# Two MLP tiles of three chunks first, a reordered opening, and loads in order of need, in a fused attention and MLP kernel

## The chip, the cores and the metric

The kernel runs on one core of a Trainium2 chip. The metric is the device time of one execution in microseconds. Most executions of one kernel agree within a few tenths of a per cent, but some fall into a slower state. The word "span" is the length of one profiled execution, and it is about 2 us shorter than the time.

The five engines have these names in the profile: PE is the matrix engine (TensorE), PEld its weight load, DVE is VectorE, ACT is ScalarE and POOL is GpSimd. SP (SyncE) issues some of the DMAs.

## The reference

Lightning attention with a decay for each head, in blocks of 64 positions, feeds a two-layer MLP with an ELU between its layers.

```python
# q, k, v: [B=4, H=8, S=768, D=64];  w_in: [512, 2048];  w_out: [2048, 512]
for b in range(nb):                                # blocks along S, kv_state carried
    intra = (qb @ kb.T) * Dmask                    # lam ** (i - j) where i >= j, else 0
    intra = intra @ vb
    inter = (qb * lam_pow) @ kv_state
    out[..., block, :] = intra + inter
    kv_state = lam_block * kv_state + (kb * rev_pow).T @ vb
x = out.transpose(0, 2, 1, 3).reshape(3072, 512)
h = x @ w_in
g = where(h > 0, h, exp(min(h, 0)) - 1)
return g @ w_out                                   # [3072, 512], float32
```

## The kernel before

The kernel takes blocks of 128 positions, which gives the same result. A "chunk" is 128 of the 3072 rows of `x`, so there are 24 chunks, 6 for each of the 4 sequences (`NCB = 6`). The MLP works on tiles of 2 to 4 chunks. A tile is 16 "slots", one for each 128 columns of the hidden layer. One slot is: the first matmul `mm1` into PSUM; `exp` and `relu` of it on ScalarE; `g = min(e - 1, r)` on VectorE; and, two slots later (`LAG = 2`), the second matmul `mm2`. The attention of the next tile's chunks is put between these, in given slots.

```python
TILES = [3, 4, 4, 4, 4, 3, 2]          # chunks of each MLP tile
# G1 = 3: chunks of tile 0.  G2 = 7: chunks of tiles 0 and 1.  NB = 8: buffers of q, k, v
...
def att_kd(g, eng):                    # k * decay; on GpSimd from tile 2 on
    ...
    kd = asb.tile([128, H, 64], FP16, tag="kd", name=f"kd{g}", bufs=3)
    ...
        eng.tensor_tensor(out=dst, in0=src, in1=ks[:]..., op=ALU.mult)

def att_q(g):                          # q * decay, in place, on GpSimd
    qt = nats[g][0]
    nc.gpsimd.tensor_tensor(out=qt[:], in0=qt[:], in1=qp[:]..., op=ALU.mult)

def att_T_dma(g):                      # transposes of q and k by DMA, from tile 2 on
    qt = asb.tile([128, NHP, 128], FP16, tag="qT", name=f"qT{g}", bufs=3)
    z = asb.tile([128, NHP, 2, 128], FP16, tag="kz", name=f"kz{g}", bufs=3)
    nc.sync.dma_start_transpose(out=qt[:], in_=nats[g][0][:]...)
    nc.sync.dma_start_transpose(out=z[:]..., in_=kn[g % NB][:]...)
...
def elu(s, e, r):                      # both inputs are in SBUF
    nc.vector.scalar_tensor_tensor(
        out=g[:, :w], in0=e, scalar=-1.0, in1=r, op0=ALU.add, op1=ALU.min)
...
for t in range(2, NMT):                # chunks from tile 2 on
    for c in range(TILES[t]):
        g, f = T0[t] + c, (t - 1) * NFT + off + step * c       # f: slot of its attention
        regular(g, f)
        prep.append((f - 6, lambda g=g: (att_q(g), att_kd(g, nc.gpsimd), att_T_dma(g))))
        prep.append((f - 16, lambda g=g: emit_load(g)))
# the other weight and chunk loads are put in `prep` at slots -3 and -2
...
for i in range(NB):                    # before slot 0
    nc.scalar.memzero(kn[i][:, :, 1:3, :])
```

The tiles `kn[i]` hold k with a zero half beside each head, so that one transpose gives a zero-padded result. Loads write the even parts and the `memzero` writes the rest. All loads that cast to 16 bits are issued by GpSimd. A load into `kn`, `vz` or `qn` has to wait until the chunk that used this buffer eight chunks earlier is done with it.

## Time and profile before

| | before |
|---|---|
| median time | 243.7 us (243.2 to 244.4) |
| span of the profiled execution | 241.3 us |
| PE busy | 212.7 us (88%) |
| first `exp` of slot 16 | 65.5 us |

From the page of before: the first line is the busy time of each engine with its share of the span and its instruction count. Each of the others has 40 equal slices of the span (6.03 us each); a digit is a share in tenths.

```profile
PE 212.7 (88%) x1444; PEld 120.5 (50%) x1444; DVE 164.8 (68%) x381; ACT 147.6 (61%) x335; POOL 121.1 (50%) x146
...
PE   1377799960989999999999999999999999999992
...
PEclk9999999996799999999999999999999999999999
DMA  6999999999999997977999999318830009200302
```

PE is full from the eleventh slice on. Before that it has one hole, in the ninth and tenth slices, and in this hole the granted clock (PEclk) falls.

The table of stretches of before gives each engine's busy time in a stretch of the span. The last three lines are tiles 1 to 3, more or less.

```profile
core 0: us, PE busy (x) PEld busy (x) DVE busy (x) ACT busy (x) POOL busy (x), PEclk, DMA share, GB/s
...
55.00:60.00 5.00, 0.13 (x2) 0.13 (x3) 0.00 (x0) 0.19 (x1) 5.00 (x7) 0.64 1.85 139
...
65.00:99.00 34.00, 32.94 (x224) 17.73 (x223) 27.69 (x62) 20.16 (x38) 29.60 (x33) 1.00 1.62 140
99.00:132.00 33.00, 32.99 (x222) 17.60 (x221) 25.79 (x55) 21.37 (x46) 17.72 (x19) 1.00 1.11 114
132.00:165.00 33.00, 32.77 (x213) 17.12 (x210) 22.42 (x45) 21.73 (x47) 16.16 (x18) 1.00 1.10 115
```

The hole in the opening comes from GpSimd's queue of loads. The timeline of POOL in before has the start, the length, the engine, the line, the operation and, in brackets, the idle time before it and what ended that. GpSimd's multiplies for chunk 7 come behind the last weight load, at 51.4 us:

```profile
50.51 0.88 POOL L108 DMA_DIRECT2D vz_78<-in_v_dram  x1 [0.75 <-DMA wo_7_133<-in_moe_w_out_dram]
51.41 1.06 POOL L233 TENSOR_TENSOR qn_409<-qn_409,qp 128x512 f16<-128x512 f16 x1
52.42 1.04 POOL L225 TENSOR_TENSOR kd_668<-kn_92,ks 128x512 f16<-128x512 f16 x1
```

The DMA transpose of that chunk follows, and PE waits for it, as the timeline of PE in before shows:

```profile
59.87 0.39 PE L333 MATMUL psSU_0_885<-qT_670,kz_671 128*128 128x128 f16 x2 [5.88 <-DMA kz_671<-kn_92]
```

From 82 us on the two multiplies of a chunk do not stand together, though twice `kd` of one chunk and `q` of the next do, as here at 118.05. Timeline of POOL in before, and below it timeline of DVE in before:

```profile
114.16 1.09 POOL L233 TENSOR_TENSOR qn_1471<-qn_1471,qp 128x512 f16<-128x512 f16 x1
118.05 1.04 POOL L225 TENSOR_TENSOR kd_1768<-kn_85,ks 128x512 f16<-128x512 f16 x1 [2.80 <-PE psSU_3_1694 L339]
119.05 1.49 POOL L233 TENSOR_TENSOR qn_1591<-qn_1591,qp 128x512 f16<-128x512 f16 x1
120.49 0.94 POOL L108 DMA_DIRECT2D qn_1885<-in_q_dram  x1
```

### The profile page before, as it was taken

What the parts mean: (1) busy time and instruction counts of PE and PEld (TensorE: products, weight loads), DVE (VectorE), ACT (ScalarE), POOL (GpSimd) and SP (SyncE); (2) the same over time, 40 slices, a digit from 0 to 9 for tenths busy, and PEclk for the clock granted to TensorE, in tenths of its full rate; (3) what the DMA queues carried; (4) which work ended last, traced back from release to release, by engine and by line L of the source; (5) the groups of instructions that cost most, each with busy time, mean ns of one, the idle gap of its engine ahead of it and who ended that gap; (6) DMA issues with size and microseconds to landing.
All of it is one profiled execution on the core that took longest, in us unless ns stands there. A gap on an engine that the chain in (4) does not pass through costs nothing.

```text
span 241.3 us, 4272 instructions
## 1 busy us (share of the span) xinstructions
PE 212.7 (88%) x1444; PEld 120.5 (50%) x1444; DVE 164.8 (68%) x381; ACT 147.6 (61%) x335; POOL 121.1 (50%) x146
## 2 busy tenths in 40 slices
PE   1377799960989999999999999999999999999992
PEld 0266565640545555555555455555455545555660
DVE  7465698770697887667888886548776739654542
ACT  6728666571265665687555656777556575667771
POOL 7987869789999885307578646053400000000000
PEclk9999999996799999999999999999999999999999
DMA  6999999999999997977999999318830009200302
GB/s 44 119 157 175 193 158 199 179 147 131 146 161 208 154 101 74 128 220 101 53 100 105 114 230 149 65 17 56 244 62 4 0 0 216 26 0 3 130 1 87
DMA packets 112373, 26.89 MB, mean 111 GB/s; under 512 B 103136, under 2 KB 109280, under 8 KB 112352
## 3 DMA queue, kind: packets, MB, share of 16 engines
q0 software_dynamic: 81552, 13.64, 79.1%
q1 hardware_dynamic: 30800, 12.99, 27.8%
q8 instruction: 11, 0.18, 0.3%
q14 instruction: 10, 0.08, 0.1%
HBM read 27.27 MB, written 6.29 MB: 139 GB/s over the span
## 4 chain that ended last, share of the span: by engine, by line
PE 67%; DMA 13%; POOL 10%; DVE 5%; issue 3%; ACT 1%; SPq 0%; DVEq 0%; ACTq 0%; POOLq 0%
DMA vz_82<-in_v_dram 4%; DMA wo_7_133<-in_moe_w_out_dram 4%; DMA wo_1_127<-in_moe_w_out_dram 4%; DMA kz_671<-kn_92 2%; PE psM_3_1503 L436 1%; PE psM_1_1026 L436 1%; PE psM_1_2416 L436 1%; PE psM_3_2418 L436 1%; PE psM_1_1501 L436 1%; PE psM_2_1502 L436 1%; PE psM_2_2417 L436 1%; PE psM_2_1027 L436 1%; PE psM_0_1500 L436 1%; PE psM_3_1028 L436 1%; PE psM_0_2415 L436 1%
## 5 line engine op out<-in xcount | busy, mean ns | idle before, releaser
L409 PEld LDWEIGHTS <-wi_7_125 128*128 128x128 f16 x56 | 5.7, 102 | 6.3 <-issue 0.9
L409 PEld LDWEIGHTS <-wi_1_119 128*128 128x128 f16 x56 | 5.3, 97 | 6.7 <-issue 2.1
L409 PEld LDWEIGHTS <-wi_3_121 128*128 128x128 f16 x56 | 5.4, 98 | 5.3
L409 PEld LDWEIGHTS <-wi_5_123 128*128 128x128 f16 x56 | 5.4, 98 | 5.3
L409 PEld LDWEIGHTS <-wi_4_122 128*128 128x128 f16 x56 | 5.4, 98 | 5.0
L409 PEld LDWEIGHTS <-wi_2_120 128*128 128x128 f16 x56 | 5.3, 98 | 4.8
L409 PEld LDWEIGHTS <-wi_6_124 128*128 128x128 f16 x56 | 5.3, 98 | 4.8
L409 PEld LDWEIGHTS <-wi_0_118 128*128 128x128 f16 x56 | 5.3, 98 | 4.7
L225 POOL TENSOR_TENSOR kd_1650<-kn_92,ks 128x512 f16<-128x512 f16 x1 | 1.0, 1042 | 11.0 <-PE psSU_3_1577 L339 11.0
L225 POOL TENSOR_TENSOR kd_2450<-kn_90,ks 128x512 f16<-128x512 f16 x1 | 1.0, 1042 | 10.8 <-issue 10.8
L333 PE MATMUL psSU_0_885<-qT_670,kz_671 128*128 128x128 f16 x2 | 0.4, 300 | 5.9 <-DMA kz_671<-kn_92 5.9
L414 ACT ACTIVATE e_903<-psH_898 128x384 f32<-128x384 f32 x1 | 0.5, 490 | 7.8 <-PE psH_898 L409 7.8
L260 PE MATMUL psT_193<-ident_138,qn_134 128*128 128x128 f16 x4 | 0.6, 308 | 5.1 <-DMA qn_134<-in_q_dram 5.1
L108 POOL DMA_DIRECT2D kn_92<-in_k_dram x6 | 4.5, 764 | 0.8 <-DMA wi_2_120<-in_moe_w_in_dram 0.6
L225 POOL TENSOR_TENSOR kd_2653<-kn_91,ks 128x512 f16<-128x512 f16 x1 | 1.0, 1043 | 6.8 <-issue 6.8
L345 DVE TENSOR_TENSOR pp_0_889<-psSU_0_885,mask 128x256 f16<-128x256 f32 x1 | 0.4, 425 | 5.8 <-PE psSU_0_885 L339 5.8
L374 PEld LDWEIGHTS <-vz_79 128*128 128x128 f16 x24 | 2.6, 112 | 2.8 <-issue 0.9
L333 PEld LDWEIGHTS <-kz_671 128*128 128x128 f16 x8 | 0.7, 114 | 6.1 <-DMA kz_671<-kn_92 6.1
L374 PEld LDWEIGHTS <-vz_84 128*128 128x128 f16 x24 | 2.3, 98 | 2.8 <-DVE xt_583 L395 0.5
L374 PEld LDWEIGHTS <-vz_81 128*128 128x128 f16 x24 | 2.3, 98 | 2.5
L374 PEld LDWEIGHTS <-vz_80 128*128 128x128 f16 x24 | 2.3, 98 | 2.5
L374 PEld LDWEIGHTS <-vz_82 128*128 128x128 f16 x24 | 2.3, 98 | 2.5
(1734 smaller groups left out, 881.8 us busy)
## 6 DMA issues: line engine op xcount, KB each, us to landing
vz_77<-in_v_dram POOLq DMA_DIRECT2D x3, 128.0 KB, 5.5
vz_78<-in_v_dram POOLq DMA_DIRECT2D x3, 128.0 KB, 5.1
vz_79<-in_v_dram POOLq DMA_DIRECT2D x3, 128.0 KB, 4.9
vz_80<-in_v_dram POOLq DMA_DIRECT2D x3, 128.0 KB, 6.2
vz_81<-in_v_dram POOLq DMA_DIRECT2D x3, 128.0 KB, 6.8
vz_82<-in_v_dram POOLq DMA_DIRECT2D x3, 128.0 KB, 8.7
kn_92<-in_k_dram POOLq DMA_DIRECT2D x6, 64.0 KB, 5.6
vz_84<-in_v_dram POOLq DMA_DIRECT2D x3, 128.0 KB, 5.4
```

What stands on the lines that cost most here:

```text
L108: nc.gpsimd.dma_start(out=dst, in_=src[:, rows].rearrange("h p d -> p h d"))
L225: eng.tensor_tensor(out=dst, in0=src, in1=ks[:].rearrange("p (g t) -> p g t", t=2).unsqueeze(3) .broadcast_to([128, NHP, 2, 64]), op=ALU.mult,
L260: nc.tensor.transpose(pt[:, j, hp, :], in_=src[:, 2 * hp : 2 * hp + 2, :], identity=ident16[:])
L333: nc.tensor.matmul(pu[:, hh * 128 : (hh + 1) * 128], lhsT=z[:, hp, hh, :], rhs=qt[:, hp, :], start=True, stop=True,)
L345: nc.vector.tensor_tensor(out=P[:], in0=pu[:, 0:256].rearrange("p (h i) -> p h i", h=2), in1=mask[:, 2 * hp : 2 * hp + 2, :], op=ALU.mult,)
L374: nc.tensor.matmul(po[:, hp, :], lhsT=vt[:, b0 : b0 + 2, :], rhs=P[:, hh, :], start=(hh == 0), stop=(hh == 1 and cb == 0), skip_group_chec ...
L409: nc.tensor.matmul(pH[:, :w], lhsT=wi[:, kk, j * 128 : (j + 1) * 128], rhs=xt[m][:, kk, :w], start=(kk == 0), stop=(kk == NHP - 1),)
L414: nc.scalar.activation(e[:, :w], pH[:, :w], AF.Exp)
L436: nc.tensor.matmul(psM[m][i][:], lhsT=g[:, i * 128 : (i + 1) * 128], rhs=wo16[wof[n][0]][:, wof[n][1], :], start=(n == 0), stop=(n == NFT ...
```

## The change

Its intent: reach the dense part sooner, by loading in the order of need and by sharing the opening's copies between ScalarE and VectorE; then let GpSimd prepare further ahead, with five buffers in place of three. The core of the diff:

```diff
-    TILES = [3, 4, 4, 4, 4, 3, 2]
+    TILES = [3, 3, 4, 4, 4, 4, 2]              # so G2 is 6
...                                             # loads, all at the start of GpSimd's queue:
-    emit_load(1)
-    emit_load(2)
+    emit_load(1, (0, 1)); emit_load(0, (2,)); emit_load(2, (0, 1)) ...
     emit_w_load(0)
     emit_load(3)
+    emit_w_load(1); emit_w_load(2); emit_load(4); emit_w_load(3); emit_w_load(4)
+    emit_load(5)
+    for i in range(5, 8):
+        emit_w_load(i)
+    emit_load(6)
+    emit_load(7)
...                                             # kd, qT (twice), kz:
-            kd = asb.tile([128, H, 64], FP16, tag="kd", name=f"kd{g}", bufs=3)
+            kd = asb.tile([128, H, 64], FP16, tag="kd", name=f"kd{g}", bufs=5)
...                                             # state of a sequence's first chunk:
-                nc.scalar.copy(new[r, r], u)
+                nc.vector.tensor_copy(new[r, r], u)
...                                             # stores, issued LAG + 2 slots later:
-                nc.sync.dma_start(out=out[t0 : t0 + 128, :], in_=o[:])
+                stores.append((s + LAG + 2, out[t0 : t0 + 128, :], o))
...
+    def pool_work(g):
+        if g + 2 < NG:
+            emit_load(g + 2)
+        att_q(g)
+        att_kd(g, nc.gpsimd)
+        att_T_dma(g)
...
-            prep.append((f - 6, lambda g=g: (att_q(g), att_kd(g, nc.gpsimd), att_T_dma(g))))
-            prep.append((f - 16, lambda g=g: emit_load(g)))
+            prep.append((f - 6, lambda g=g: pool_work(g)))
+    for i in range(NB):
+        prep.append((i, lambda i=i: nc.scalar.memzero(kn[i][:, :, 1:3, :])))
...                                             # before slot 0:
-    for i in range(NB):
-        nc.scalar.memzero(kn[i][:, :, 1:3, :])
```

Cut from it: the order of transposes, copies and mask in the opening, the PSUM tags of tile 2's attention, and the slots of each chunk. The zeroing of `kn[i]` now stands in slot `i`, behind the loads of k in the order of the program.

More of the change, by code (lines that the diff above doesn't have):

```diff
@@ L64 @@
     nc.sync.dma_start(out=lam_b[:], in_=lam.unsqueeze(0).broadcast_to([128, H]))
+    ident16 = cpool.tile([128, 128], FP16, name="ident16")
+    nc.vector.memset(ident16[:], 0.0)
+    causT = cpool.tile([128, 128], FP32, name="causT")
+    nc.vector.memset(causT[:], 1.0)
     vz = [cpool.tile([128, 2 * H, 64], FP16, name=f"vz_{i}") for i in range(NB)]
@@ L79 @@
         nc.vector.memset(kz0[i][0:64, :, 1, :], 0.0)
-    for i in range(NB):
+    for i in range(G1):
         nc.vector.memset(vz[i][:, 1::2, :], 0.0)
-    def late_zeros():
-        for i in range(G1):
-            nc.vector.memset(kdz[i][:, :, 1:3, :], 0.0)
-        for hp in range(NHP):
-            for i in range(2):
-                nc.vector.memset(st[hp][i][:], 0.0)
+        nc.vector.memset(kdz[i][:, :, 1:3, :], 0.0)
     nats = {}
@@ L132 @@
     emit_load(0, (0, 1))
-    ident16 = cpool.tile([128, 128], FP16, name="ident16")
-    nc.gpsimd.memset(ident16[:], 0.0)
     nc.gpsimd.affine_select(
@@ L138 @@
     )
-    causT = cpool.tile([128, 128], FP32, name="causT")
-    nc.gpsimd.memset(causT[:], 1.0)
     nc.gpsimd.affine_select(
@@ L148 @@
     nc.gpsimd.iota(iota_r[:], pattern=[[1, 128]], base=0, channel_multiplier=0)
+    emit_load(1, (0, 1))
     emit_load(0, (2,))
-    emit_load(1)
-    emit_load(2)
+    emit_load(2, (0, 1))
+    emit_load(1, (2,))
+    emit_load(2, (2,))
     emit_w_load(0)
     emit_load(3)
+    emit_w_load(1)
+    emit_w_load(2)
+    emit_load(4)
+    emit_w_load(3)
+    emit_w_load(4)
+    emit_load(5)
[3 more added lines that the diff above has]
+    emit_load(7)
     loglam = cpool.tile([128, H], FP32, name="loglam")
@@ L181, with emit_mask @@
     mask = cpool.tile([128, H, 128], FP32, name="mask")
-    nc.vector.tensor_tensor(
-        out=mask[:],
-        in0=causT[:].unsqueeze(1).broadcast_to([128, H, 128]),
-        in1=dn[:].unsqueeze(2).broadcast_to([128, H, 128]),
-        op=ALU.mult,
-    )
+    def emit_mask():
+        nc.vector.tensor_tensor(
+            out=mask[:],
+            in0=causT[:].unsqueeze(1).broadcast_to([128, H, 128]),
+            in1=dn[:].unsqueeze(2).broadcast_to([128, H, 128]),
+            op=ALU.mult,
+        )
     qs = cpool.tile([128, NHP, 128], FP32, name="qs")
@@ L238, in att_T_dma @@
     def att_T_dma(g):
-        qt = asb.tile([128, NHP, 128], FP16, tag="qT", name=f"qT{g}", bufs=3)
-        z = asb.tile([128, NHP, 2, 128], FP16, tag="kz", name=f"kz{g}", bufs=3)
+        qt = asb.tile([128, NHP, 128], FP16, tag="qT", name=f"qT{g}", bufs=5)
+        z = asb.tile([128, NHP, 2, 128], FP16, tag="kz", name=f"kz{g}", bufs=5)
         nc.sync.dma_start_transpose(out=qt[:], in_=nats[g][0][:].rearrange("p h d -> p (h d)"))
@@ L265, in att_ev @@
         pt = psT.pop(g)
-        qt = asb.tile([128, NHP, 128], FP16, tag="qT", name=f"qT{g}", bufs=3)
+        qt = asb.tile([128, NHP, 128], FP16, tag="qT", name=f"qT{g}", bufs=5)
         z = kz0[g % 2]
@@ L271, in att_ev @@
             nc.scalar.copy(out=qt[:], in_=pt[:, 0])
-        for hh in range(2):
-            r = slice(hh * 64, (hh + 1) * 64)
-            nc.scalar.copy(out=z[r, :, hh, :], in_=pt[r, 1])
+        nc.scalar.copy(out=z[0:64, :, 0, :], in_=pt[0:64, 1])
+        if g < G1:
+            nc.vector.tensor_copy(z[64:128, :, 1, :], pt[64:128, 1])
+        else:
+            nc.scalar.copy(out=z[64:128, :, 1, :], in_=pt[64:128, 1])
         qkT[g] = (qt, z)
@@ L401, with emit_stores @@
     psM = {}
+    stores = []
+    def emit_stores(s):
+        while stores and stores[0][0] <= s:
+            _, dst, o = stores.pop(0)
+            nc.sync.dma_start(out=dst, in_=o[:])
     def mm1(s):
@@ L457, in regular @@
     def regular(g, f):
+        tags = ("psSU", "psM3") if T0[2] <= g < T0[3] else ("psSU", "psSU")
         for hp in range(NHP):
-            at(f + hp, lambda hp=hp: att_SU(g, hp))
+            at(f + hp, lambda hp=hp: att_SU(g, hp, tags[hp % 2]))
             at(f + 1 + hp, lambda hp=hp: att_PI(g, hp), late=hp == 0)
@@ L469, in short @@
         at(f + 2, lambda: att_X(g, 2))
-    for g, (ft, f) in zip(range(G1, G2), ((-1, 1), (3, 5), (7, 9))):
+    for g, ft, f in ((3, 0, 2), (4, 5, 7), (5, 10, 12)):
         at(ft, lambda g=g: (att_T_pe(g), att_ev(g)))
-        regular(g, f)
+        (short if g == 5 else regular)(g, f)
         prep.append((f - 1, lambda g=g: att_kd(g, nc.vector)))
-    at(12, lambda: (att_T_pe(G2 - 1), att_ev(G2 - 1)))
-    short(G2 - 1, 13)
-    prep.append((13, lambda: att_kd(G2 - 1, nc.vector)))
-    START = {4: (-2, 4), 3: (0, 5), 2: (2, 6)}
+    def pool_work(g):
[4 more added lines that the diff above has]
+        att_T_dma(g)
@@ L481 @@
     for t in range(2, NMT):
-        off, step = START[TILES[t]]
         for c in range(TILES[t]):
-            g, f = T0[t] + c, (t - 1) * NFT + off + step * c
-            regular(g, f)
-            prep.append((f - 6, lambda g=g: (att_q(g), att_kd(g, nc.gpsimd), att_T_dma(g))))
-            prep.append((f - 16, lambda g=g: emit_load(g)))
-    for s, f in (
-        (-3, lambda: emit_w_load(1)), (-3, lambda: emit_load(4)), (-3, lambda: emit_w_load(2)),
-        (-3, lambda: emit_w_load(3)), (-3, lambda: emit_load(5)), (-2, lambda: emit_w_load(4)),
-        (-2, lambda: emit_w_load(5)), (-2, lambda: emit_w_load(6)), (-2, lambda: emit_load(6)),
-        (-2, lambda: emit_w_load(7)),
-    ):
-        prep.append((s, f))
@@ L496 @@
-    prep.sort(key=lambda x: x[0])
-    PIs = lambda g: [att_PI(g, hp) for hp in range(NHP)]
-    SU = lambda g: (pre_S(g, 0), pre_P(g, 0), pre_S(g, 1), pre_P(g, 1))
+            g = T0[t] + c
+            f = (t - 1) * NFT + (2 + 3 * c if t == 2 else 6 * c if t == NMT - 1 else 4 * c - 2)
+            if t == 2 and c == 3:
+                f += 1
+                short(g, f)
+            else:
+                regular(g, f)
+            prep.append((f - 6, lambda g=g: pool_work(g)))
+    for i in range(NB):
+        prep.append((i, lambda i=i: nc.scalar.memzero(kn[i][:, :, 1:3, :])))
@@ L501, with PIs, SP @@
+    prep.sort(key=lambda x: x[0])
+    def PIs(g):
+        for hp in range(NHP):
+            att_PI(g, hp)
+    def SP(g):
+        for i in range(2):
+            pre_S(g, i)
+            pre_P(g, i)
     att_T_pe(0)
     att_ev(0)
-    late_zeros()
+    emit_mask()
+    att_kd(0, nc.vector)
+    emit_qs()
+    SP(0)
+    for hp in range(NHP):
+        for i in range(2):
+            nc.vector.memset(st[hp][i][:], 0.0)
     att_T_pe(1)
-    SU(0)
-    att_kd(0, nc.scalar)
-    emit_qs()
+    att_ev(1)
@@ L508 @@
+    for i in range(G1, NB):
+        nc.scalar.memzero(vz[i][:, 1::2, :])
+    SP(1)
     pre_U(0)
     pre_st(0)
-    att_ev(1)
-    att_T_pe(2)
-    SU(1)
     att_kd(1, nc.vector)
     PIs(0)
+    att_T_pe(2)
+    att_ev(2)
     att_X(0)
+    SP(2)
     pre_U(1)
-    att_ev(2)
     pre_st(1)
-    SU(2)
     PIs(1)
     att_X(1)
-    att_kd(2, nc.scalar)
     PIs(2)
     att_X(2, 2)
-    pre_U(2)
-    pre_st(2)
-    for i in range(NB):
-        nc.scalar.memzero(kn[i][:, :, 1:3, :])
-    for s in range(-3, NMT * NFT + LAG):
+    att_kd(2, nc.scalar)
@@ L531, with after_first @@
+    def after_first():
+        pre_U(2)
+        pre_st(2)
+    slot_ops[0].insert(0, after_first)
+    for s in range(NMT * NFT + LAG):
         while prep and prep[0][0] <= s:
             prep.pop(0)[1]()
+        emit_stores(s)
         live = 0 <= s < NMT * NFT
@@ L543 @@
             fn()
+    emit_stores(NMT * NFT + 2 * LAG)
 _INS = ['q', 'k', 'v', 'lam', 'moe_w_in', 'moe_w_out']
```

## The prediction

> **What bounds the kernel now.** After about 64 us it is TensorE: in the table of stretches PE is busy 20.0, 20.0, 19.8, 20.0, 19.7 and 20.0 us of each 20 us from 80 to 200. Before that it is the GpSimd load queue. In the timeline of POOL an issue waits for the landing of the DMA eight before it; w_out 7 is issued at 41.25 and lands at 50.0. Only then (51.4) do the two multiplies for chunk 7 run, then its two DMA transposes (kz issued 53.9, 6.0 us to land). The chain of waits runs through these. PE waits 5.9 us (53.9 to 59.9) and comes back cold: 0.43 us per 512-column matmul until 63.2, 0.22 after. That is 3.3 us of cold work; the Trainium skill, "TensorE: Matmul & The Clock Gate", "What's actually happening", gives about 3.4 us sustained, and this trace agrees. Slot 16 (tile 1's first mm1) starts at 64.4.
>
> **What the change does.**
> (a) Opening: VectorE and ScalarE share copies, q1/k1 load before v0, mask and state zeros move. From the durations (0.11 us per cold matmul, 0.42 qT copy, 0.68 mask multiply) I estimate slot 0 at 22.3 instead of 25.8.
> (b) Tile 1 has 3 chunks: chunk 6 is now first of tile 2, is needed 4 slots later, and uses DMA transposes (8 PE transposes less, 0.5 us). Other matmul work is equal.
> (c) All loads stand first on GpSimd: chunks 0 to 5, all weights, then 6, 7. From the landings before, a chunk's q, k or v costs the queue 0.95 us, a weight piece 1.2. So w_out 7 lands at about 44.3, k6 at 46.2, k7 at 49.1.
> (d) The zeros of kn[i] move to ScalarE in slot i. The order of instructions with its semaphores shows a trap: the zeroing of kn[6] in slot 6 and of kn[7] in slot 7 wait for the DMAs that load k6 and k7 into the same tiles, now issued before them (the bytes don't overlap, but the tracker orders them). ScalarE works in order, so exp/relu of slots 6 and 7 stand behind those landings, and mm1 of slots 8 and 9 behind them (two psH buffers).
>
> So I expect ScalarE at slot 6 by about 32 us, blocked until 46.3; PE starved from about 34 to 47.5; a second wait until 49.2; mm1 of slot 9 at about 50.4. All that (a) gains lies off the critical path. The transposes of chunk 6 land near 56 and are needed at slot 18 (near 66): the old 5.9 us wait disappears.
>
> **The sum.** Slots 9 to 15 at 1.7 us: slot 16 at 62.6 (before 64.4). Tile 1: 16 slots of 1.29 us plus 4 chunks' attention at 1.35, plus 1.5 for a crowded VectorE: 27.6. Three 4-chunk tiles at 33.4: 100.3. A 4-chunk tile with 2 chunks' attention: 31. Last tile and tail as before: 20.8. Span 242.3 against 241.3, since 1.5 chunks' attention less is done by slot 16. With the 2.3 us between span and time: **244.3 us, range 239.5 to 248.5**; faster by over 2% 0.13, within 2% 0.75, slower 0.12.
>
> Store queueing: 0; the waits before show none from it.
>
> **Would show it right.** ScalarE idle about 14 us before the zeroing of kn[6] and about 2 before kn[7], released by the k DMAs; a PE gap near 34 to 47; no PE wait on a kz transpose; PE full after 52.
> **Would show it wrong.** No ScalarE gap (then slot 18 waits only for kz6 near 56, and about 235 results); k7 landing early or late, which moves the end one for one; VectorE stalls in tile 1 beyond 1.5 us.

## More of the kernel before

The 1.46 us here is the longest `g` of the whole execution. By the records it stands beside nothing but load issues, while the `g` at 118.90, which begins during a multiply with another directly behind it, takes only 0.74 us and the second multiply 1.49.

```profile
118.90 0.74 DVE L422 SCALAR_TENSOR_TENSOR g_1702<-e_1687,r_1689 128x512 f16<-128x512 f32 x1
...
120.96 1.46 DVE L422 SCALAR_TENSOR_TENSOR g_1734<-e_1718,r_1720 128x512 f16<-128x512 f32 x1
```

The multiply `kd` at 118.05 waited 2.80 us for a free buffer (it has three).

## The result, and the profile after

| | before | after |
|---|---|---|
| median time | 243.7 us (243.2 to 244.4) | 252.8 us (251.6 to 253.8) |
| profiled span | 241.3 us | 251.2 us |
| PE busy | 212.7 us (88%) | 213.9 us (85%) |
| DVE busy | 164.8 us | 181.2 us |

The ratio is 1.037, with a 95% interval of 1.032 to 1.042. The change is slower. A ratio here is the mean time of one kernel's fast runs over that of the other's of the same rounds, so it is not quite the ratio of the medians.

From the page of after, the same lines as of before (a slice is 6.28 us):

```profile
PE 213.9 (85%) x1436; PEld 119.0 (47%) x1436; DVE 181.2 (72%) x404; ACT 140.5 (56%) x304; POOL 124.9 (50%) x147
...
PE   1466891499899978799898988999999999999992
...
PEclk9999897599999999999999999999999999999998
```

PE's busy time is nearly that of before. The hole has moved to an earlier place (the seventh and eighth slices), and there are new shallow holes, digits 7 and 8, through the part that was full before. The table of stretches of after has the same columns as that of before:

```profile
40.00:45.00 5.00, 0.00 (x0) 0.00 (x0) 0.00 (x0) 0.00 (x0) 3.54 (x5) 0.60 1.91 174
...
65.00:97.00 32.00, 28.13 (x219) 16.66 (x217) 29.53 (x72) 16.73 (x40) 31.03 (x34) 1.00 2.15 144
97.00:132.00 35.00, 32.47 (x212) 16.95 (x210) 29.56 (x54) 20.16 (x39) 25.86 (x30) 1.00 1.72 130
132.00:168.00 36.00, 33.86 (x222) 17.75 (x222) 29.74 (x62) 20.14 (x38) 13.21 (x14) 1.00 0.79 96
```

PE idles 3.9 us in tile 1 (65 to 97), 2.5 us in tile 2 and 2.1 us in tile 3 (the length less the busy time). In before each of the three loses at most 1.1 us. DVE has become busier: 29.56 us with 54 instructions in the stretch of tile 2, against 25.79 us with 55 in before. Time in which an instruction is held up counts as busy here.

**The early hole.** Timeline of ACT in after:

```profile
36.18 0.58 ACT L286 COPY kz<-psT 64x512 f16<-64x512 f16 x1
45.93 0.42 ACT L515 ACTIVATE kn<-kn 128x256 uint32<-128x256 uint32 x1 [9.18 <-DMA kn<-in_k_dram]
46.37 0.49 ACT L432 ACTIVATE e<-psH 128x384 f32<-128x384 f32 x1
...
48.94 0.42 ACT L515 ACTIVATE kn<-kn 128x256 uint32<-128x256 uint32 x1 [1.69 <-DMA kn<-in_k_dram]
```

L515 is the zeroing of `kn[i]`. ScalarE works in order, so everything behind the zeroing of `kn[6]` stands 9.18 us until the load of k for chunk 6 has landed in the same tile. PE then has nothing to do, as the timeline of PE in after shows:

```profile
37.82 0.81 PE L454 MATMUL psM<-wo,g 128*128 128x512 f16 x3
47.30 1.12 PE L427 MATMUL psH<-xt,wi 128*128 128x384 f16 x3 [8.66 <-DMA kn<-in_k_dram]
```

The order of instructions with their semaphores says the same without a run. It is no view of the profile. DMASW3 and DMASW4 are the lanes of the two loads of k for chunk 6, the other two those for chunk 7:

```text
L515 Activation kn_6_95<-kn_6_95 128x4x64 [waits DMASW4_49,DMASW3_49]
L515 Activation kn_7_96<-kn_7_96 128x4x64 [waits DMASW7_49,DMASW0_49]
```

**The shallow holes.** Timeline of POOL in after, and below it timelines of DVE and of PE for the same moment:

```profile
146.27 0.89 POOL L107 DMA_DIRECT2D vz<-in_v_dram  x1 [3.74 <-PE psSU L351]
147.17 1.06 POOL L243 TENSOR_TENSOR qn<-qn,qp 128x512 f16<-128x512 f16 x1
148.18 1.05 POOL L235 TENSOR_TENSOR kd<-kn,ks 128x512 f16<-128x512 f16 x1
149.18 1.04 POOL L243 TENSOR_TENSOR qn<-qn,qp 128x512 f16<-128x512 f16 x1
```

```profile
146.58 0.58 DVE L371 SCALAR_TENSOR_TENSOR st<-st,upp,psSU 64x64 f16<-64x64 f16 x2
147.19 3.58 DVE L440 SCALAR_TENSOR_TENSOR g<-e,r 128x512 f16<-128x512 f32 x1
150.81 0.42 DVE L357 TENSOR_TENSOR pp<-psSU,mask 128x256 f16<-128x256 f32 x1
```

```profile
151.29 0.27 PE L386 MATMUL psO<-pp,vz 128*128 128x128 f16 x2 [1.30 <-DVE pp L357]
```

Three multiplies stand in a row on GpSimd from 147.17 to 150.22, and one `g` takes 3.58 us from 147.19 to 150.77. It ends 0.55 us after the last multiply ends. The chain of waits of after (start, length, what) runs through it:

```profile
146.87 0.30 DVE st L371
147.17 0.02 issue
147.19 3.60 DVE g L440
150.79 0.02 issue
150.81 0.42 DVE pp L357
```

There are four such waits between 119 and 151 us: 3.06 us (at 119.54), 2.59 (129.07), 1.78 (138.94) and 3.58 (147.19). Each `g` ends 0.55 to 0.57 us after the last multiply. The groups of after by shape (busy us in all, mean ns) show what this sums to; the right part is the idle time before the group. The last two lines are from the table of waits of after, over the whole span (us in total, times, longest):

```profile
L440 DVE SCALAR_TENSOR_TENSOR g<-e,r 128x512 f16<-128x512 f32 x64 | 55.6, 869 | 18.1 <-ACT r L434 16.7
...
L440 DVE SCALAR_TENSOR_TENSOR g<-e,r 128x384 f16<-128x384 f32 x32 | 26.2, 819 | 15.1 <-ACT r L434 14.5
...
POOL vz L107 <- PE psSU L351: 16.6, 5, 4.2
PE psO L386 <- DVE pp L357: 3.6, 7, 1.3
```

The timing is no accident. In after, GpSimd runs as far ahead as the buffers of v allow: the load of v for chunk `g + 2` waits until chunk `g - 6` is done with the buffer, and that is a PE instruction (the 3.74 us wait at 146.27). The load takes 0.89 us, and then the multiplies begin. VectorE is released by the same PE instruction, does `pp` (0.42 us) and `st` (0.58 us), and then begins `g`, within half a microsecond of the first multiply. So it is in three of the four; the `g` at 138.94 begins 0.83 us after the first multiply.

Standing together is not enough. Seven more pairs in after, from 65 us on, have a `g` that begins before the first multiply ends (at 65.31, 70.99, 80.97, 86.65, 92.31, 104.44 and 154.33), and none of these stands behind a load that had waited. There `g` ends before the second multiply does and takes at most 1.59 us; it is the second multiply that takes longer, 1.40 to 1.55 us in place of 1.05. The four pairs or rows with the long `g` are just those behind a load that had waited 3.74 to 4.16 us for PE. What decides whether `g` gets its turn between two multiplies no run here shows.

**Where the 10 us are.** The table compares tile lengths, measured from first `exp` to first `exp` in the timelines of ACT. In before tile 1 has four chunks and tile 5 three, in after it is the other way round, so tile 1 and tile 5 of these two rows are not directly comparable. All others of one column have equal MLP work, but not always equal attention in it. The lengths are of one profiled execution each; where nothing between the kernels should change them they agree well (c1 and c2 to 0.01 us in tiles 1 to 3; after, d1 and g1 to 0.4 us).

| kernel | slot 16's `exp` at | tile 1 | tile 2 | tile 3 | tile 4 | tile 5 | median time | ratio to before (95%) |
|---|---|---|---|---|---|---|---|---|
| before | 65.5 | 33.6 | 32.9 | 32.7 | 32.0 | 24.3 | 243.7 | |
| after | 64.8 | 32.1 | 35.0 | 36.2 | 32.8 | 30.0 | 252.8 | 1.037 (1.032 to 1.042) |
| c1_no_mult | 65.4 | 29.5 | 32.7 | 33.2 | 32.8 | 30.0 | 244.0 | 1.005 (1.001 to 1.010) |
| a1_zero_early | 53.1 | 33.9 | 34.3 | 35.3 | 32.8 | 30.0 | 241.6 | 0.998 (0.991 to 1.006) |
| e1_bufs3 | 65.4 | 31.1 | 33.4 | 33.7 | 32.9 | 30.0 | 248.6 | 1.023 (1.020 to 1.026) |
| i1_before_bufs5 | 66.4 | 34.3 | 32.9 | 32.6 | 31.8 | 24.3 | 245.0 | 1.006 (1.000 to 1.011) |
| i2_before_bufs5_order | 64.4 | 33.8 | 34.6 | 34.7 | 31.8 | 24.3 | 247.2 | 1.018 (1.014 to 1.022) |
| d1_copies_act | 65.1 | 32.4 | 34.7 | 36.3 | 32.6 | 30.0 | 253.0 | 1.039 (1.036 to 1.042) |
| g1_stores_now | 64.3 | 32.1 | 34.6 | 36.2 | 32.8 | 30.0 | 253.0 | 1.037 (1.031 to 1.043) |
| f1_zero_bufs3 | 52.8 | 33.9 | 34.3 | 33.7 | 32.9 | 30.0 | 239.9 | 0.986 (0.982 to 0.991) |
| h1_zero_split | 51.9 | 35.6 | 33.4 | 34.8 | 32.8 | 30.0 | 239.2 | 0.982 (0.976 to 0.987) |
| c2_zero_no_mult | 52.4 | 29.5 | 32.7 | 33.2 | 32.8 | 30.0 | 232.7 | 0.957 (0.953 to 0.960) |
| k1_zero_q_first | 51.8 | 30.7 | 32.8 | 33.7 | 32.8 | 30.0 | 235.7 | 0.966 (0.960 to 0.970) |

The medians of i1, g1 and k1 include their slow runs; over the fast runs alone they are 244.8, 252.0 and 234.3 us. One run of before at 451.7 us was slow too and is left out.

The predicted terms were slot 16's `mm1` at 62.6 us, 27.6 us for tile 1, 100.3 us for tiles 2 to 4, 31 us for tile 5 and 20.8 us for the rest. Measured were 64.0, 32.1, 103.9 (35.0 + 36.2 + 32.8), 30.0 and, as what is left of the span, 21.2. The differences are +1.4, +4.5, +3.6, -1.0 and +0.4, together the +8.9 us between the predicted span of 242.3 and the measured one of 251.2.

### The profile page after: what moved, and what is told of

Same layout as the page of the kernel before. It is cut to its first block, busy times and chain, and to the rows that moved or that the text cites. A ratio compares the mean times of both kernels' runs of the same rounds, so it can differ in the third digit from the quotient of the medians.

```text
span 251.2 us, 4251 instructions
## 1 busy us (share of the span) xinstructions
PE 213.9 (85%) x1436; PEld 119.0 (47%) x1436; DVE 181.2 (72%) x404; ACT 140.5 (56%) x304; POOL 124.9 (50%) x147
## 4 chain that ended last, share of the span: by engine, by line
PE 53%; DVE 23%; DMA 12%; POOL 5%; issue 4%; ACT 1%; POOLq 0%; DVEq 0%; ACTq 0%
PE psH L427 23%; PE psM L454 23%; DVE g L440 11%; DMA wo<-in_moe_w_out_dram 6%; DVE st L371 5%; DVE pp L357 4%; DMA vz<-in_v_dram 4%; PE psSU L345 3%; PE psO L386 2%; DMA kn<-in_k_dram 2%; DVE osb L462 2%; POOL qn L107 2%; POOL vz L107 1%; POOL kf L107 1%; ACT r L434 1%
## 5 line engine op out<-in xcount | busy, mean ns | idle before, releaser
L440 DVE SCALAR_TENSOR_TENSOR g<-e,r 128x512 f16<-128x512 f32 (+2 forms) x112 | 88.7, 792 | 40.3 <-ACT r L434 38.2
L427 PE MATMUL psH<-xt,wi 128*128 128x512 f16 (+2 forms) x448 | 103.0, 353 | 9.6 <-DMA kn<-in_k_dram 8.7
L432 ACT ACTIVATE e<-psH 128x512 f32<-128x512 f32 (+2 forms) x112 | 60.2, 537 | 84.2 <-PE psH L427 84.1
L454 PE MATMUL psM<-wo,g 128*128 128x512 f16 x384 | 103.2, 381 | 3.1 <-DVE osb L462 2.7
L427 PEld LDWEIGHTS <-wi 128*128 128x128 f16 x448 | 43.5, 99 | 52.7 <-issue 12.8
L434 ACT ACTIVATE r<-psH 128x512 f16<-128x512 f32 (+2 forms) x112 | 59.7, 533 | 0.0
L454 PEld LDWEIGHTS <-g 128*128 128x128 f16 x384 | 34.1, 98 | 26.2 <-issue 4.3
L357 DVE TENSOR_TENSOR pp<-psSU,mask 128x256 f16<-128x256 f32 x84 | 35.4, 423 | 14.4 <-PE psSU L351 8.8
L371 DVE SCALAR_TENSOR_TENSOR st<-st,upp,psSU 64x64 f16<-64x64 f16 x112 | 30.8, 275 | 1.6
L386 PE MATMUL psO<-pp,vz 128*128 128x128 f16 x192 | 25.8, 224 | 6.5 <-DVE pp L357 3.6
L386 PEld LDWEIGHTS <-vz 128*128 128x128 f16 x192 | 18.6, 100 | 25.8 <-issue 9.1
L107 POOL DMA_DIRECT2D kn<-in_k_dram x36 | 27.2, 765 | 1.1 <-DMA wi<-in_moe_w_in_dram 0.8
L515 ACT ACTIVATE kn<-kn 128x256 uint32<-128x256 uint32 x8 | 3.4, 422 | 10.9 <-DMA kn<-in_k_dram 10.9
```

The source lines that it names most:

```text
L107: nc.gpsimd.dma_start(out=dst, in_=src[:, rows].rearrange("h p d -> p h d"))
L357: nc.vector.tensor_tensor(out=P[:], in0=pu[:, 0:256].rearrange("p (h i) -> p h i", h=2), in1=mask[:, 2 * hp : 2 * hp + 2, :], op=ALU.mult,)
L371: nc.vector.scalar_tensor_tensor(out=new[r, r], in0=old[r, r], scalar=upp[r, hp : hp + 1], in1=u, op0=ALU.mult, op1=ALU.add,)
L386: nc.tensor.matmul(po[:, hp, :], lhsT=vt[:, b0 : b0 + 2, :], rhs=P[:, hh, :], start=(hh == 0), stop=(hh == 1 and cb == 0), skip_group_chec ...
L427: nc.tensor.matmul(pH[:, :w], lhsT=wi[:, kk, j * 128 : (j + 1) * 128], rhs=xt[m][:, kk, :w], start=(kk == 0), stop=(kk == NHP - 1),)
L432: nc.scalar.activation(e[:, :w], pH[:, :w], AF.Exp)
```

## The experiments

Eleven kernels were run, each against before on the same chip in the same rounds. Two of them give a wrong result on purpose (c1 and c2), all others are correct.

The theory after the result: GpSimd's multiplies, when they stand together, hold up VectorE's `g`, and this costs PE time in tiles 1 to 3. The Trainium skill, page "SBUF — State Buffer", section "Who interferes with whom", says: "A DVE instruction with two SBUF inputs contends with a GpSimd instruction that reads SBUF, not with one that only writes it". `g` has two SBUF inputs and the multiplies read SBUF. The rivals: the copies of the state that moved to VectorE crowd it; the queued stores hold something up; the loads in the background do.

### a1_zero_early: the zeroing of kn[6] and kn[7] ahead of their loads

```diff
+    for i in range(G2, NB):
+        nc.scalar.memzero(kn[i][:, :, 1:3, :])
     emit_load(6)
     emit_load(7)
...
-    for i in range(NB):
+    for i in range(G2):
         prep.append((i, lambda i=i: nc.scalar.memzero(kn[i][:, :, 1:3, :])))
```

> The changed kernel with one edit: the zeros of kn[6] and kn[7] are written on ScalarE at the start, before the loads of k6 and k7 are issued. Stall theory: ScalarE no longer waits 9.2 and 1.7 us; slots run on to slot 18, which waits for the DMA transpose of chunk 6 (about 57 us instead of slot 18 at 66.6), so about 8 to 10 us less than the changed kernel: 243 to 245 us. If the stall was hidden behind something else the time stays at 252 to 253. Shared-port and crowded-VectorE theories say the same here: tiles 1 to 3 stay long (about 32, 35 and 36 us from first exp to first exp).

Measured: the hole is gone. Slot 16's `exp` is at 53.1 us in place of 64.8, and the ratio to before falls from 1.037 to 0.998. So the stall cost after 3.9% (about 9.4 us of 243.5, with an interval of some 2 us to each side). I had expected 243 to 245 us; 241.6 is faster than that. In the profiled executions the spans differ by 11.5 us (251.2 and 239.7): slot 16 comes 11.8 us sooner, tile 1 is 1.9 us longer (33.9 against 32.1), and tiles 2 and 3 are 0.7 and 0.8 us shorter. In tile 1 of a1 GpSimd is busy without a gap, and PE waits 2.4 us for two transposes of k. So GpSimd seems to have too little lead there; this is read from the waits of a1 and was not isolated.

### c1_no_mult: GpSimd's multiplies taken out (wrong)

```diff
     def pool_work(g):
         if g + 2 < NG:
             emit_load(g + 2)
-        att_q(g)
-        att_kd(g, nc.gpsimd)
+        if g % NCB != NCB - 1:
+            kds[g] = kn[g % NB]            # undecayed k in place of kd
         att_T_dma(g)
...
-                lhsT=kds[g][:, 2 * hp : 2 * hp + 2, :],
+                lhsT=(kds[g][:, hp, 0:2, :] if g >= G2
+                      else kds[g][:, 2 * hp : 2 * hp + 2, :]),
```

> The changed kernel with the two GpSimd multiplies per chunk taken away from chunk 6 on (results wrong on purpose; the matmuls read other bytes of the same tiles). Shared-port theory: no VectorE g longer than 0.8 us for 512 columns or 0.65 for 384; tile 1 (first exp to first exp) 32.1 -> 29 or less, tiles 2 and 3 35.0 and 36.2 -> 33 or less; time about 243 to 245. Crowded-VectorE theory (four chunks' attention in a 3-chunk tile, state copies moved to VectorE): tile 1 stays at 31 or more, tiles 2 and 3 at 34.5 or more; time 250 to 253.

Measured: 1.005 against after's 1.037, so the multiplies cost 3.15% or 7.7 us. The tiles 1 to 3 lose 2.6, 2.3 and 2.9 us of their length, 7.8 us in all (at 29.5 and 33.2 us tiles 1 and 3 stay a little above the 29 and 33 that I had expected). Tiles 4 and 5, in which GpSimd has run out of multiplies, are the same. The groups of c1 by shape show that no `g` is held up:

```profile
L440 DVE SCALAR_TENSOR_TENSOR g<-e,r 128x512 f16<-128x512 f32 x64 | 44.3, 692 | 18.3 <-ACT r L434 16.7
...
L440 DVE SCALAR_TENSOR_TENSOR g<-e,r 128x384 f16<-128x384 f32 x32 | 17.8, 557 | 17.1 <-ACT r L434 16.4
```

c1 also takes work off GpSimd, so it could have gained by earlier loads and transposes instead. The waits in the two traces speak against that: in tiles 1 to 3 of after PE waits 7.5 us for VectorE, 1.0 us for ScalarE and for no DMA and nothing of GpSimd's; in c1 it waits 1.5 us for VectorE and the same 1.0 us for ScalarE.

The longest `g` of c1 is 0.694 us, though GpSimd still issues all its loads and VectorE works beside them. So in c1 issuing loads alone stretches no `g`. This agrees with the second half of the skill's sentence, if an issue reads no SBUF, which no run here shows. In kernels that do have the multiplies the records are less clear: before's `g` of 1.46 us at 120.96 and others of up to 1.53 us (a1) stand beside nothing but load issues. GpSimd's records are rough, and what held these up stays open. The long ones, of 1.78 us and more in tiles 2 and 3, all stand beside multiplies. Slot 16 is at 65.4 us, so the early hole has nothing to do with the multiplies.

### e1_bufs3: three buffers again

```diff
-            kd = asb.tile([128, H, 64], FP16, tag="kd", name=f"kd{g}", bufs=5)
+            kd = asb.tile([128, H, 64], FP16, tag="kd", name=f"kd{g}", bufs=3)
...                                             # the same for qT (twice) and kz
```

> The changed kernel with 3 buffers again (not 5) for kd, qT and kz, so that GpSimd's kd multiply is held back by its own buffer as before and stands apart from the q multiply. Shared-port theory: in tiles 2 and 3 the longest g falls from 3.6 us to under 1.6 and the tiles from 35.0 and 36.2 to about 33; tile 1 changes less; time 247 to 249. Crowded-VectorE theory: no change, 252 to 253.

Measured: 1.023, where after has 1.037. Tiles 2 and 3 are 1.6 and 2.5 us shorter, and their longest `g` is 1.49 us. The wait for a third buffer holds most of the `kd` multiplies back (by 1.8 to 9.7 us in tiles 2 and 3) and so parts them from the `q` multiplies. The fifth buffer, which was meant as a gain, is one of the conditions of the loss.

### i1_before_bufs5: the five buffers alone, in before

```diff
-            kd = asb.tile([128, H, 64], FP16, tag="kd", name=f"kd{g}", bufs=3)
+            kd = asb.tile([128, H, 64], FP16, tag="kd", name=f"kd{g}", bufs=5)
...                                             # the same for qT (twice) and kz, in before
```

> The kernel before with only one part of the change: 5 buffers for kd, qT and kz. Shared-port theory: GpSimd runs further ahead until the v buffer holds it, its two multiplies come back to back, g instructions of 2 us and more appear between 64 and 165 us, and the time rises by 2 to 5 us to 246 to 249. Crowded-VectorE theory: within 0.5 us of 243.7.

Measured: 245.0 us, 1.006 (1.000 to 1.011; one of its runs was slow and is left out). This missed: I had expected 246 to 249. The five buffers alone cost almost nothing. Over tile 1 its `g` instructions take 6.3 us more than they would undisturbed, in waits of at most 0.9 us each (3.9 us of it beside load issues alone, by the records). In before the same tile has 2.6 us of such waits, so 3.7 us more made it only 0.7 us longer. So the sum of what VectorE loses does not tell the cost. One `g` of 3.24 us stands at 50.83, before tile 1; in the stretch that I had named, from 64 to 165 us, none takes more than 1.6 us.

### i2_before_bufs5_order: the five buffers and GpSimd's new order, in before

```diff
+    def pool_work(g):
+        if g + 2 < NG:
+            emit_load(g + 2)
+        att_q(g); att_kd(g, nc.gpsimd); att_T_dma(g)
...
-            prep.append((f - 6, lambda g=g: (att_q(g), att_kd(g, nc.gpsimd), att_T_dma(g))))
-            prep.append((f - 16, lambda g=g: emit_load(g)))
+            prep.append((f - 6, lambda g=g: pool_work(g)))
+            if g < G2 + 2:
+                prep.append((f - 16, lambda g=g: emit_load(g)))
...                                             # and bufs=5 as in i1
```

> The kernel before with 5 buffers (as i1) and also the changed kernel's order on GpSimd: the load two chunks ahead always directly before the two multiplies. If this pair of parts makes the loss (v load released by TensorE, then both multiplies at the moment that VectorE starts g), g instructions of 2.5 us and more appear in the stretches from slot 32 to 64, these grow from 32.9 and 32.7 to 34 or more, and the time is 246 to 248. If not, about 245 as i1.

Measured: 247.2 us, 1.018. Tiles 2 and 3 are 1.7 and 2.1 us longer than in i1, although the tiles, the opening and the zeroing are those of before. The timelines of POOL and DVE in i2 show the same picture as those of after:

```profile
129.12 0.89 POOL L108 DMA_DIRECT2D vz<-in_v_dram  x1 [3.74 <-PE psSU L339]
130.02 1.06 POOL L233 TENSOR_TENSOR qn<-qn,qp 128x512 f16<-128x512 f16 x1
131.03 1.05 POOL L225 TENSOR_TENSOR kd<-kn,ks 128x512 f16<-128x512 f16 x1
```

```profile
130.04 2.60 DVE L422 SCALAR_TENSOR_TENSOR g<-e,r 128x512 f16<-128x512 f32 x1
```

So the load directly ahead of the pair makes the difference; what fits the traces is that it ties the pair to a PE instruction. The five buffers let it happen, the order makes it happen.

### d1_copies_act: the state copies back on ScalarE

```diff
-                nc.vector.tensor_copy(new[r, r], u)
+                nc.scalar.copy(new[r, r], u)
```

> The changed kernel with the state copies of a sequence's first chunk on ScalarE again (24 copies of about 0.22 us leave VectorE). Crowded-VectorE theory: tile 1 (first exp to first exp) falls by about 1 us from 32.1, and the time by 1 to 2 us from the changed kernel's 252 to 253 (ratio to before about 1.030). Shared-port theory: no more than 0.7 us, ratio 1.034 to 1.039, and the long g instructions stay (2.6 us and more in tiles 2 and 3).

Measured: 1.039 (1.036 to 1.042), which is not to be told from after; tile 1 is 32.4 us, no shorter. The rival of crowding by these copies falls.

### g1_stores_now: the stores issued at once

```diff
-                stores.append((s + LAG + 2, out[t0 : t0 + 128, :], o))
+                nc.sync.dma_start(out=out[t0 : t0 + 128, :], in_=o[:])
```

> The changed kernel with the output stores issued at once after their evictions, as before, instead of queued behind later transposes. As predicted, store queueing is worth nothing: ratio to before within 0.004 of the changed kernel's 1.037. If the queueing helps, this run is slower by 1 us or more; if it is part of the loss, faster by 1 us or more.

Measured: 1.037 (1.031 to 1.043; one slow run is left out), the same as after. Queueing the stores is worth nothing here in either direction, as predicted.

### f1_zero_bufs3: a1 and e1 together

```diff
...                                             # a1's early zeroing, and bufs=3 as in e1
```

> The changed kernel with both repairs: early zeros (as in a1) and 3 buffers (as in e1). If the two losses are separate they add: a1's 241.6 less the 3 to 4 us that e1 gained on the changed kernel: 237.5 to 239.5, ratio to before about 0.98. If the early zeros only moved the load on, so that 3 buffers now delay chunk 7 and later, it stays at 241 or more.

Measured: 239.9 us, 0.986 (0.982 to 0.991). I had expected at most 239.5, so it is missed by 0.4 us. The buffers gained 1.6 us in tile 3 (33.7 against 35.3 in a1) but nothing in tiles 1 and 2, whose lengths are those of a1 to a tenth. My reading is that GpSimd has no lead there that three buffers could take away.

### h1_zero_split: a1, with the load of v between the two multiplies

```diff
     def pool_work(g):
-        if g + 2 < NG:
-            emit_load(g + 2)
+        if g + 2 < NG:
+            emit_load(g + 2, (0, 1))
         att_q(g)
+        if g + 2 < NG:
+            emit_load(g + 2, (2,))
         att_kd(g, nc.gpsimd)
         att_T_dma(g)
...                                             # and a1's early zeroing
```

> Early zeros, 5 buffers, but on GpSimd the q multiply stands before the v load (which is what waits for TensorE) and the kd multiply after it, so the two multiplies are never neighbours. Shared-port theory: no g longer than 1.7 us, tiles 2 and 3 at 33.0 to 33.8 instead of a1's 34.3 and 35.3, time 238 to 240. If the cause were the number of multiplies and not their standing together, the tiles stay at 34 to 35 and the time at 241 to 242.

Measured: 239.2 us, 0.982. Tile 2 improved to 33.4 us, but tile 3 took 34.8 us where I had expected 33.0 to 33.8. Its longest `g` is 2.67 us, at 135.68. There the last load of v, which had waited 3.69 us for PE, has just been issued (no chunk `g + 2` is left after it), so only the multiplies remain on GpSimd, and `kd` of one chunk and `q` of the next stand together again, at 135.73 and 136.74. Separating the multiplies works as long as there is something to put between them. Tile 1 became longer, 35.6 us against 33.9 in a1: PE waits there 2.8 us for one transpose of k (2.4 us for two in a1) and once 1.2 us for a state on VectorE.

### c2_zero_no_mult: a1 and c1 together (wrong)

```diff
...                                             # a1's early zeroing, and c1's edit
```

> Early zeros and no GpSimd multiplies from chunk 6 on (wrong on purpose): the floor with both losses gone. If they are separate, the 11 us of a1 and the 9 us of c1 add up: 232 to 234. If something else holds the stage from slot 18 on (the DMA transposes, crowded VectorE), 236 or more.

Measured: 232.7 us, 0.957 (0.953 to 0.960). This is what the change would give with neither cost. From after's 1.037 to 0.957 it is 8.0% of before, or 19.5 us. The two parts measured alone are 3.9% and 3.15%; the 1.0% by which their sum falls short is within the uncertainty of the four ratios (about 1.1%), so that the two costs simply add is not contradicted.

### k1_zero_q_first: a correct version that uses this

```diff
     def pool_work(g):
-        if g + 2 < NG:
-            emit_load(g + 2)
         att_q(g)
+        att_T_dma(g)
+        if g + 2 < NG:
+            emit_load(g + 2, (0, 1))
         att_kd(g, nc.gpsimd)
-        att_T_dma(g)
+        if g + 2 < NG:
+            emit_load(g + 2, (2,))
...                                             # and a1's early zeroing
```

> Early zeros, 5 buffers; on GpSimd for each chunk first the q multiply and the two DMA transposes, then the q and k loads two chunks ahead, then the kd multiply, then the v load. Multiplies never neighbours, and the transposes of chunk 6 start about 4 us sooner (near 47 instead of 50 to 51.5). Shared-port theory and the a1 reading together: no PE wait on a kz transpose over 1 us, no g over 1.7 us, 236 to 238.5, ratio to before about 0.975. If the order of GpSimd does not matter, 239 to 241.6 as f1, h1 and a1.

Measured: 235.7 us (234.3 over the fast runs), 0.966 (0.960 to 0.970), with correct results (two slow runs are left out of the ratio). That is faster than the 0.975 that I had expected. It beats before by 3.4% and after by 6.9% (0.966 over 1.037). The transposes no longer stand behind `kd`, and loads stand between the two multiplies, as the timeline of POOL in k1 shows:

```profile
97.10 1.08 POOL L237 TENSOR_TENSOR kd<-kn,ks 128x512 f16<-128x512 f16 x1
98.09 0.95 POOL L107 DMA_DIRECT2D vz<-in_v_dram  x1
99.06 1.06 POOL L245 TENSOR_TENSOR qn<-qn,qp 128x512 f16<-128x512 f16 x1
```

In tiles 2 and 3 no `g` takes more than 1.53 us, and the tiles are 2.2 and 2.5 us shorter than in after. PE waits only 0.2 us for a transpose of k. Tile 1 is 3.2 us shorter than in a1; k1 makes both changes at once, the earlier transposes and the parted multiplies, and how they share this gain was not separated.

## Why the prediction was wrong

**What was right.** The trap of the zeroing was read from the order of instructions, and the trace has it almost to the tenth of a microsecond: ScalarE starts again at 45.93 us (predicted 46.3) and the second zeroing begins at 48.94 (49.2); slot 9's `mm1` starts at 50.6 (50.4). The ends of the PE hole are 38.6 and 47.3 (34 and 47.5). The start was estimated too early, as ScalarE reached slot 6 at 36.8 (36.18 + 0.58) and not at 32; this costs nothing, because only the end of the hole counts. That the gains of the opening lie off the critical path holds: slot 0's first `mm1` comes at 23.5 us instead of 25.8 (predicted 22.3), and slot 16 is still late. a1 shows what held it: with the zeroing out of the way slot 16 comes 11.8 us sooner. That the old 5.9 us wait for a transpose disappears holds, and that the stores are worth nothing too (g1). PE is slow at first after the hole, as it was after the hole of before (four matmuls of 384 columns take 1.44 us together at 47.30 and 0.81 at 53.00). In before this lasted 3.3 us, from 59.87 to 63.2; the Trainium skill, "TensorE: Matmul & The Clock Gate", section "What's actually happening", gives about 3.4 us.

**What was wrong: the steps "plus 1.5 for a crowded VectorE: 27.6" and "Three 4-chunk tiles at 33.4: 100.3".** The prediction has no term for the five buffers and for GpSimd's new order in the steady part. They put two or three SBUF-reading multiplies of GpSimd side by side, at the moment at which VectorE starts `g`. The prediction had itself named "VectorE stalls in tile 1 beyond 1.5 us" as a sign that it was wrong; PE waits 2.9 us for VectorE there. What the runs showed in place of these two terms:

- Tile 1 took 32.1 us, 4.5 more. Without the multiplies (c1) it takes 29.5. So 2.6 us of the miss are the multiplies. The other 1.9 us are mostly PE's own work, put too low: in tile 1 of c1 PE is busy for 27.7 us (the ends of matmuls are modelled in the profile), where 16 slots of 1.29 us and 4 chunks at 1.35 had made 26.0. A crowded VectorE is not the reason for them, since PE waits only 0.8 us for VectorE in tile 1 of c1, less than the 1.5 us allowed.
- Tiles 2 to 4 took 103.9 us, 3.6 more. Without the multiplies they take 98.7, so my 33.4 each was 1.6 us too much in all, and the multiplies added 5.2 us to tiles 2 and 3. The longest `g`s took 3.06, 2.59 and 3.58 us.

**Why not before.** In before most multiplies stood apart; the five pairs that stood together from 62 us on were not behind a load that had waited for PE, and the longest `g` was 1.46 us. The i1 run shows that even five buffers do not change this (1.006). With the new order, too, it does (i2, 1.018). With three buffers back, after's loss falls from 3.7% to 2.3% (e1).

**The other terms.** From slot 9's `mm1` to slot 16's took 13.4 us (50.6 to 64.0) where I had put 12.2 (50.4 to 62.6), so slot 16 was 1.4 us late. c1 has slot 16 no earlier, so the multiplies are not the cause. PE is busy for 12.9 of these 13.4 us in after, so here too PE's own work was put too low. Tile 5 was 1.0 us faster than I had put, the tail 0.4 us slower. The time exceeds the span by 1.7 us in after, where I had added 2.3.

**What stays open.** What decides whether a `g` waits for one multiply or for the whole row; what held up the `g`s beside which the records show only load issues; and how much of a1's longer tile 1 is GpSimd's own pace and how much VectorE's waits.

The Trainium skill had a warning of this: its page "SBUF — State Buffer", section "Who interferes with whom", names the two kinds of instruction that collide, though not what it would cost. I knew both instructions from the kernel and did not ask when they would run at the same time.

## What to carry to other kernels

When a change moves an engine's work or gives it more buffers, ask not only what comes earlier but which instructions will now stand side by side, and whether another engine starts a conflicting one on the same release. The sum of waits does not tell their cost: in tile 1 of i1 3.7 us more of short waits than in before cost 0.7 us, while single `g`s of 2.6 to 2.8 us (waits of about 2 us) cost tiles 2 and 3 of i2 1.7 and 2.1 us. Short waits are not free everywhere, though: tile 1 of the changed kernel has 4.4 us of waits of at most 1.0 us each, and it is 2.6 us longer than in c1. And before zeroing part of a tile that a load also fills, put the zeroing ahead of the load in the order of the program.

## What the Trainium skill lacked or had wrong

- "SBUF — State Buffer", section "Who interferes with whom", says of VectorE's 2-port modes that whoever issues first gets the shared pair for the whole instruction and that the other blocks. What happens to a waiting VectorE instruction when GpSimd has several in a row is not on the page. The runs show both outcomes. In four places of after a `g` was kept waiting through all of the row: it took 2.59 us past two multiplies (i2 has 2.60) and 3.58 us past three, each ending 0.55 to 0.57 us after the last of them. In seven other places of after it got its turn between two, took at most 1.59 us, and the second multiply took 1.40 to 1.55 us.
- The same section lets issue order decide. At 119.54 us in after a `g` whose record starts 0.44 us before the first multiply (119.98) still took 3.06 us, while that multiply took its usual 1.06 us. The start in the record of a VectorE instruction is thus not what decides who waits.
- The same page's "not with one that only writes it" agrees with c1: beside nothing but load issues no `g` took more than 0.694 us. Beside records of load issues alone a `g` took up to 1.53 us in kernels that also have the multiplies; no run here explains this.
- No page says how such a wait turns into time. Tile 1 of i1 has 6.3 us of waits of at most 0.9 us, 3.7 us more than in before, and is 0.7 us longer; `g`s of 2.6 to 2.8 us made tiles 2 and 3 of i2 1.7 and 2.1 us longer than in i1.
